# Two chunks of 96 tokens, casts of weights on GpSimd, packs formed turned, and new urgencies in a fused attention and MLP kernel

## The chip, the cores and the metric

The kernel runs on one core of a Trainium2 chip. The metric is the time of one launch on the device, in microseconds; the figure before is the median of three runs.

## The reference

Eight batches, eight heads, 576 tokens, head size 64, and 32 learned packs p per head. Attention runs twice: the packs attend to the tokens, which gives 32 packed vectors per head, and the tokens attend to those. Then comes an MLP over the 4608 tokens with the heads side by side (512 wide, 2048 inside):

```python
p_packed = sm_attn(p, k, v)               # softmax(p k^T / 8) v
out = sm_attn(q, p_packed, p_packed)      # softmax(q packed^T / 8) packed
x = out.transpose(0, 2, 1, 3).reshape(B * S, H * D)
h = x @ w_in
g = h * erf(softplus(h))
return g @ w_out
```

q, k, v and p are float32, the two weights float64 in memory.

## The kernel before

The kernel never forms x. With packs P and the token weights A of the second softmax, x @ w_in is A @ (P @ w_in): it makes "wp" = P @ w_in once for each batch and quarter of the 2048 columns (`w_prime`, `w_prime_first`), and then h = A @ wp, unit by unit; a unit is one batch and 128 of the 2048 columns (`h_unit`). To keep float32 precision at the fast rate, an operand is split into a high part (rounded to the fast float type) and a low part (the rest), and each product is three products: high x high, high x low, low x high. The tiles are named hi/lo, gh/gl, woh/wol, wph/wpl, a2h/a2l.

The first two batches run g @ w_out plainly, as units of "o". From the third batch on the same is done with fewer products by a scheme of sums and differences of blocks (`block`, products "c"), from parts of w_out that were formed before and kept in memory (`parts`).

The float64 weights are loaded as 16-bit words and turned into float32 in three steps (`convert`): GpSimd clears the target (L424), an engine casts the upper halves into it (L425 on ScalarE or L426 on VectorE, whichever comes first), and VectorE shifts the rest into place (L427). The staging tiles are wos (for w_out), wi and w_in. The first quarter of w_in comes in four pieces (`load_w_in_pair`): x says which half of the columns, and 2 * i which rows.

The first batch (`attention(0, ...)`, then `direct`) is the head of the kernel. Its order is: load p and k, queries, values; scores s of the packs (L421 called from `landed`); maximum and exponential; turn the weights (transposes, L699, L704) into tiles a1t and a1r; multiply them with the values (`gather`, tile p, 80 instructions); scale by the sums, transpose, copy: the packs pt (L738 to L743). The second scores (q against pt) follow, and `direct` handles their softmax in three parts of 256, 256 and 64 tokens.

What stands in which order is set by a planner in the kernel's own Python (`Program.order`). Every operation has a key, its urgency: where several are ready on an engine, the one with the lowest key goes first. The planner plays the whole program through with assumed durations, and the order that comes out is fixed for each engine's queue. Loads go to SyncE's queue, and they too are taken by lowest key, as far as there is room in their tiles. For the first batch the keys are -40 + i + PLAN["first"][i]: i = 0 for p and k, 1 for the values, 2 for the queries, 7 for the turns, 8 for the packs, 9 for the second scores, 10 to 13 for the parts of its softmax. A piece of w_in has the key of the values plus PLAN["first w"][2 * x + i].

At the end of `tile_pack_attention_moe` a loop fills TensorE's planned idle time before its operations with products of an identity matrix that nobody reads ("fill"), which are then part of TensorE's order. A wide one is two instructions of 512 columns.

The last block ends with two halves d = 0, 1: each is 12 products, one sum on VectorE (L1136) and two transfers, one on SyncE's queue and one on ScalarE's (L1141).

Of the kernel before, what the change touches and what calls it, by code (L numbers as in the profile page):

```python
# [14 lines left out]
F16 = mybir.dt.float16  # L15
BF16 = mybir.dt.bfloat16
# [5 lines left out]
PLAN = {  # L22
    "first": (-1655.04, -1082.68, -1274.99, 79.58, 0.0, 35.36, 16.66, 31.53, 72.43, 139.69, 67.61, -31.88, 85.8, 31.26),
    "wi by piece": (-162.72, 49.43, 320.21),
    "conv by piece": (89.72, -291.66, -190.3),
    "wo by group": (-551.62, -435.73, -397.6, -90.41, 49.67),
    "wo conv by group": (198.37, 226.24, -12.57, 1007.38, -374.69),
    "soon": (40.49, 61.86, -122.56, -117.47, -4.12, 109.39, 55.24, -94.6, 129.63, 109.4),
    "lag": 19.03,
    "act": -1381.6,  # L30
    "dve": -5.97,
    "copy": -21.32,
    "steady": (-77.6, 18.81, -15.19, -109.95, -11.8, 63.04, 10.58, -48.44, -142.04, 70.31, -139.34, -47.51, -66.75, 134.23),
    "second": (-53.98, -74.8, -47.15, -104.65, 87.68, -26.81, 73.19, -53.86, 5.68, -257.33, -25.4, 72.87, 198.79, -223.82),
    "third": (-46.13, 18.51, 43.92, 63.5, -111.16, 133.27, 18.45, 122.84, -270.72, 41.02, 42.6, -48.71, -122.17, -142.57),
    "wp": -78.11,
    "wi": 524.6,
    "wo": 108.98,
    "conv": -22.0,
    "rest": 27.37,  # L40
# [3 lines left out]
    "second half": 41.53,  # L44
    "wp first": (46.87, 23.46),
    "late": 1.436,
    "first w": (-34.02, 599.89, 20.85, -124.83),
    "also": {'top': -158.75, 'gate': 68.38, 'h': -0.92, 'cast': 81.65, 'taken': 21.33, 'h fast': -1157.74},
    "fill": (1.4, 60.0, 0.3, 0.4),
    "pad": (1.0, 0.0, 0.155, 0.079),  # L50
    "behind": 0.0,
    "first conv": (-145.98, -39.44, -15.82, -187.66),
# [3 lines left out]
    "split": 109.59,  # L56
# [12 lines left out]
    "gate": (-154.21, 1428.56, 1589.98),  # L69
    "copy fast": 34.59,  # L70
    "wp fast": -1007.0,
    "steady fast": (69.72, 75.09, 83.13, 101.05, 35.66, -202.52, -143.36, 7.84, -47.88, -22.2, -195.85, 216.61, -167.61, 61.46),
    "ml": (39.51, 1.95, 453.11),
    "sums ahead": (-103.94, 96.56, 110.02, -86.04, -59.16, -18.04, 88.79, 18.91, 4.56),
    "last ahead": (-78.59, -143.94, 85.03),
    "take": (14.93, -1376.66, -22.16),
    "fetch": -11.79,
    "st lead": (123.79, -10.21, 27.06, 147.95),
# [1282 lines left out]
```

## Time and profile before

| | us |
|---|---|
| median of 3 runs | 688.31 (687.78 to 689.96) |
| profiled execution | 687.53 |
| its span | 685.8 |
| TensorE busy | 674.9 (98%) |
| VectorE busy | 586.6 (86%) |
| ScalarE busy | 534.5 (78%) |
| GpSimd busy | 48.8 (7%) |

The span goes from the first to the last instruction of the profiled execution; its own time is that of the launch. Busy time counts an engine as soon as one of its instructions runs. For TensorE it holds the fillers too, and overlapping instructions count once. Idle time of an engine on which nobody waits costs nothing.

### The profile page before, as it was taken

To read this page: it belongs to the slowest core of one execution; us is meant where nothing else is said; L and a number is where in the kernel's file an instruction comes from. 1 tells how busy PE (TensorE), PEld (TensorE's weight loads), DVE (VectorE), ACT (ScalarE), POOL (GpSimd) and SP (SyncE) were. 2 spreads that over 40 slices of the span, in tenths; PEclk is the share of its full clock that TensorE was granted. 3 is DMA by queue.
4 is the path that set the end of the run, shared out by engine and by line. 5 is a ranking of instruction groups with operands and counts; after the bars stand their busy time and mean duration, and the time that the engine had idled before them with its cause. 6 is when DMAs were issued, how large, how long until landed. Compare 5 with 4: busy or idle time off the path is not lost.

```text
span 685.8 us, 15245 instructions
## 1 busy us (share of the span) xinstructions
PE 674.9 (98%) x5942; PEld 601.0 (88%) x5942; DVE 586.6 (86%) x990; ACT 534.5 (78%) x854; POOL 48.8 (7%) x67
## 2 busy tenths in 40 slices
PE   8999999999999999999999999999999999999997
PEld 4676778898769899898999989899998989999997
DVE  2899888978676899969999798969989699968995
ACT  2699699999369788877888787976889778868851
POOL 7200000001020000010001100011000100002000
PEclk9999999999999999999999999999999999999999
DMA  9999877997993796879769897779858787978973
GB/s 318 383 359 330 257 244 244 308 304 237 303 259 109 280 350 204 268 220 349 235 205 307 239 312 244 235 227 315 296 195 285 201 248 225 336 199 241 367 259 85
DMA packets 91288, 181.45 MB, mean 265 GB/s; under 512 B 16976, under 2 KB 46416, under 8 KB 91216
## 3 DMA queue, kind: packets, MB, share of 16 engines
q1 hardware_dynamic: 83904, 171.45, 73.1%
q0 software_dynamic: 6864, 8.29, 8.5%
q8 instruction: 47, 0.77, 0.5%
q10 hardware_dynamic: 448, 0.74, 0.3%
q14 instruction: 25, 0.20, 0.1%
HBM read 140.86 MB, written 39.58 MB: 263 GB/s over the span
## 4 chain that ended last, share of the span: by engine, by line
PE 86%; DVE 5%; ACT 3%; DMA 3%; issue 1%; POOL 0%; DVEq 0%; ACTq 0%; POOLq 0%
PE c L421 38%; PE h L421 26%; PE o L421 10%; PE wp L421 4%; PE s L421 3%; DMA wos<-w_out 2%; PE fill_ps_h L421 1%; PE p L421 1%; DMA wi<-w_in 1%; PE or L421 1%; PE t L699 1%; DVE gl L1030 1%; DVE hs L947 1%; DVE x L947 0%; ACT L942 0%
## 5 line engine op out<-in xcount | busy, mean ns | idle before, releaser
L421 PE MATMUL c<-gh,st 128*128 128x288 f32 x1344 | 286.1, 297 | 1.0 <-ACT obr L1165 0.7
L421 PEld LDWEIGHTS c<-gh,st 128*128 128x128 f32 x1344 | 220.7, 188 | 12.4 <-DVE cb L1088 3.9
L421 PE MATMUL c<-gl,st 128*128 128x288 f32 x672 | 198.2, 295 | 0.0
L421 PE MATMUL h<-a2h,wph 128*128 128x288 f32 (+2 forms) x512 | 154.7, 303 | 1.9 <-ACT hs L993 0.9
L421 PE MATMUL h<-a2l,wph 128*128 128x288 f32 (+2 forms) x512 | 150.6, 295 | 0.0
L421 PE MATMUL h<-a2h,wpl 128*128 128x288 f32 (+2 forms) x512 | 150.4, 294 | 0.0
L421 PEld LDWEIGHTS c<-gl,st 128*128 128x128 f32 x672 | 126.2, 188 | 0.0
L1030 DVE TENSOR_TENSOR gl<-x,gh 128x576 fp32r<-128x576 f32 x144 | 105.5, 749 | 3.4 <-ACT gh L1028 3.4
L421 PEld LDWEIGHTS h<-a2h,wph 128*128 128x128 f32 x512 | 95.9, 188 | 11.5 <-ACT hs L993 3.3
L421 PEld LDWEIGHTS h<-a2l,wph 128*128 128x128 f32 x512 | 96.1, 188 | 1.4 <-issue 0.5
L421 PEld LDWEIGHTS h<-a2h,wpl 128*128 128x128 f32 x512 | 96.2, 188 | 0.0
L1028 ACT CAST gh<-x 128x576 fp32r<-128x576 f32 x103 | 67.6, 672 | 35.6 <-PE c L421 30.5
L993 ACT COPY x<-h 128x288 f32<-128x288 f32 x117 | 46.6, 399 | 45.0 <-PE h L421 42.4
L995 DVE COPY x<-h 128x288 f32<-128x288 f32 x75 | 34.1, 454 | 29.4 <-PE h L421 29.0
L1097 POOL DMA_DIRECT2D out_t<-cb x21 | 25.4, 1208 | 444.9 <-DVE cb L1083 190.6
L1088 DVE TENSOR_TENSOR cb<-cb,c 128x576 f32<-128x576 f32 x59 | 44.2, 749 | 12.6 <-PE c L421 12.6
L421 PE MATMUL o<-woh,gh 128*128 128x512 f32 x120 | 48.0, 400 | 0.0
L421 PE MATMUL o<-woh,gl 128*128 128x512 f32 x120 | 46.9, 391 | 0.0
L421 PE MATMUL o<-wol,gh 128*128 128x512 f32 x120 | 46.8, 390 | 0.0
L942 ACT ACT_TABLE_LOAD x36 | 46.2, 1283 | 0.6
L937 ACT ACT_TABLE_LOAD x36 | 46.2, 1283 | 0.6
L1022 DVE TENSOR_TENSOR x<-x,x 128x576 f32<-128x576 f32 x48 | 35.8, 747 | 0.0
(430 smaller groups left out, 1078.7 us busy)
## 6 DMA issues: line engine op xcount, KB each, us to landing
st<-parts SPq DMA_DIRECT2D x167, 512.0 KB, 5.2
q<-qT SPq DMA_DIRECT2D x32, 288.0 KB, 5.8
k<-kT SPq DMA_DIRECT2D x30, 288.0 KB, 5.7
v<-v SPq DMA_DIRECT2D x32, 256.0 KB, 5.5
wos<-w_out SPq DMA_DIRECT2D x16, 511.8 KB, 5.0
out_t<-cb SPq DMA_DIRECT2D x26, 288.0 KB, 4.0
wi<-w_in SPq DMA_DIRECT2D x12, 511.8 KB, 6.1
out_t<-cb POOLq DMA_DIRECT2D x21, 288.0 KB, 6.4
```

The lines of the kernel that those rows point to most:

```text
L421: return nc.tensor.matmul(*args, **kw)
L699: return [nc.tensor.transpose(tbanks[x]()[:, (j % 2 * 2 + r) * P:(j % 2 * 2 + r + 1) * P], a[:, r, j * P:(j + 1) * P], ident[:]) for j in ...
L937: done.append(act(n + k0, S, lambda t=t, hs=hs: nc.scalar.activation(t[:], hs[:], AF.Softplus), (t,), (hs,), run="softplus", sb=True, kind ...
L942: erfs.append(act(e + k1 + i, S, lambda t=t: nc.scalar.activation(t[:], t[:], AF.Erf), (t,), (), run="erf", sb=True, kind=int(i < len(grou ...
L947: dve(key, S, lambda t=t, hs=hs: nc.vector.tensor_tensor(hs[:], t[:], hs[:], op=ALU.mult), (hs,), (t,))
L993: op = act(n + c / 2 - PLAN["copy" if b < NS else "copy fast"] + (PLAN["soon"][8 + (n > 7)] if n < 16 else 0), n1, lambda to=to, ps=ps, t0 ...
L995: also("h" if b < NS else "h fast", op, "DVE", dve_us(n1), lambda to=to, ps=ps, t0=t0, t1=t1, n1=n1: nc.vector.tensor_copy(to[:, t0:t1], p ...
L1022: dve(key, S, lambda: nc.vector.tensor_tensor(out[:], x[:], y[:], op=op), (out,), [t for t in (x, y) if t is not out])
L1028: op = act(key, S, lambda: nc.scalar.copy(hi[:], x[:]), (hi,), (x,), sb=True)
L1030: dve(key, S, lambda: nc.vector.tensor_tensor(lo[:], x[:], hi[:], op=ALU.subtract), (lo,), (x, hi))
L1088: dve(mk(s, 1) - PLAN["take"][one], S, lambda: nc.vector.tensor_tensor(two(out), two(x), to[:, :, 0:HT], op=ALU.add), (out,), (to,) if out ...
L1097: dma(mk(s, 1), P * S * 4, lambda: nc.gpsimd.dma_start(dst, two(t), accum_op=ALU.add), (), (t,), "POOL", after=[written[b, half, c]])
```

## The change

- The 576 tokens were cut into four chunks of 128 and one of 64 for the product with the values; now they are three of 128 and two of 96.
- In `convert` the cast of the upper halves can go to GpSimd: for quarters 1 to 3 of w_in and rows 2 to 15 of w_out. ScalarE is the other engine that may take it.
- In the first batch the weights are turned in three pieces, each as soon as its exponential is there. The product with the values is also formed turned (`gather_turned`, tile pq), which gives the packs already in the layout that the second scores need, without scaling. The scale by the sums goes into the copies of the second scores. The old form (`gather`) is kept for wp, with its key raised by "packs late".
- The identity is made by two instructions, of which the second is now the first in GpSimd's fixed order.
- The planner's start of the loads, their lateness, and the pace of the fillers (two paces) are set anew.
- The first half of the last sum is put ahead of the second half's products in the order of emission (`ahead`).
- The numbers of PLAN are new.

```diff
-    "first": (-1655.04, -1082.68, -1274.99, 79.58, 0.0, 35.36, 16.66, 31.53, 72.43, 139.69, 67.61, -31.88, 85.8, 31.26),
+    "first": (-1908.15, -1140.06, -1169.28, -122.78, 0.0, -54.09, 45.51, 65.33, -30.15, 122.75, 116.35, 23.39, 192.53, 145.43),
...
+    "packs late": 71.0,
+    "turned early": -112.1,
+    "by pool": (1, 2),
+    "pool lead": -185.41,
+    "pool other": 73.85,
...
-    "first w": (-34.02, 599.89, 20.85, -124.83),
+    "first w": (-24.06, -9.19, 29.08, -85.21),
-    "fill": (1.4, 60.0, 0.3, 0.4),
+    "fill": (2.0, 5.2, 50.0, 0.3, 0.4),
...
-        state = {"table": None, "within": False, "kind": 0, "bus": 2.3, "sent": 0}
+        state = {"table": None, "within": False, "kind": 0, "bus": 1.8, "sent": 0}
...
+            if op.ahead:
+                op.start = min(op.start, op.ahead.start - 1e-6)
...
+    LEFT = (S - (NT - 1) * P) // 2
+    CHUNKS = [(j * P, P) for j in range(NT - 1)] + [(S - 2 * LEFT, LEFT), (S - LEFT, LEFT)]
...
-    make_identity(nc, ident.t)
+    nc.gpsimd.memset(ident[:], 0.0)
+    line("POOL", nc.gpsimd.affine_select(out=ident[:], in_=ident[:], compare_op=ALU.not_equal, fill=1.0, base=0,
+                                         pattern=[[-1, P]], channel_multiplier=1))
...
+        if pool:
+            op = prog.add("POOL", key - PLAN["pool lead"], 0.25 + 0.00105 * n, 0.2, lambda: line("POOL", nc.gpsimd.tensor_copy(
+                dst().bitcast(F16)[:, 1::2], words().bitcast(BF16)[:, 2::4])), w, r)
+            op.other = ("ACT", PLAN["pool other"], act_us(n * 1.37, True), lambda: line("ACT", nc.scalar.copy(
+                dst().bitcast(F16)[:, 1::2], words().bitcast(BF16)[:, 2::4])))
...
+        pieces_of = ((0, 0, NT, (0, 0)), (1, 0, 2, (1, 0)), (1, 2, NT, (1, 1)))
...
+        if first:
+            for i, (r, j0, j1, part) in enumerate(pieces_of):
+                pe(keys[7] + i / 8, 0.11 * (j1 - j0), lambda r=r, j0=j0, j1=j1: [
+                    nc.tensor.transpose(tbanks[r]()[:, j * P:(j + 1) * P], a[:, r, j * P:(j + 1) * P], ident[:]) for j in range(j0, j1)],
+                   ((tw[r], part),), ([(a, 0)], [(a, (1, 0))], [(a, (1, 0)), (a, (1, 1))])[i] + [ident])
...
+            def gather_turned(j):
+                n = CHUNKS[j][1]
+                return [mm(turned[64 * r:64 * r + 64, NK * c:NK * c + NK],
+                           values[j][0:n, 64 * (2 * c + r):64 * (2 * c + r) + 64],
+                           at[0:n, j, r, NK * c:NK * c + NK] if j < NT else ar[0:n, r * P + NK * c:r * P + NK * c + NK],
+                           start=(j == 0 and c == 0), stop=(j == NCH - 1), skip_group_check=True)
+                        for c in range(NC) for r in range(2)]
+            for j in range(NCH):
+                pe(keys[8] + j / 8, V_US / 5, lambda j=j: gather_turned(j), (turned,),
+                   [(at, (0, 0)), (at, (1, j // 2)), values[j]] if j < NT else [ar, values[j]])
+            op = dve(keys[8], P, lambda: nc.vector.tensor_copy(early[:], turned[:, 0:P]), (early,), (turned,))
+            also("packs", op, "ACT", act_us(P), lambda: nc.scalar.copy(early[:], turned[:, 0:P]))
+            pe(keys[8] + PLAN["packs late"], V_US, lambda: gather(range(NCH)), ((w[0], "o"),),
+               [(at, part) for _, _, _, part in pieces_of] + [ar] + values)
+            keys = list(keys)
+            keys[8] += PLAN["packs late"]
...
-                act(keys[9] + x / 16, t1 - t0, lambda banks=banks, t0=t0, t1=t1, r=r: nc.scalar.copy(
-                    flat(ta)[:, 2 * t0 + r * (t1 - t0):2 * t0 + (r + 1) * (t1 - t0)], banks[r]()[:, 0:t1 - t0]),
-                    ((ta, (x, r)),), (w[r],))
+                act(keys[9] + x / 16, t1 - t0, lambda banks=banks, t0=t0, t1=t1, r=r: nc.scalar.activation(
+                    flat(ta)[:, 2 * t0 + r * (t1 - t0):2 * t0 + (r + 1) * (t1 - t0)], banks[r]()[:, 0:t1 - t0],
+                    AF.Copy, scale=sums[:, r:r + 1]), ((ta, (x, r)),), (w[r], (sums, r)))
...
+            op.ahead = halves.get(d + 1)
...
         while t + 0.112 < op.start - margin:
-            n = next((n for n in (4, 2) if t + 0.224 * n < op.start - margin - 0.5), 1)
+            one = 0.22 if t < slow else 0.112
+            n = next((n for n in (4, 2) if t + 2 * n * one < op.start - margin - 0.5), 1)
```

## Rows read from the trace of the kernel before

**Rows 1.** Busy us (instructions) by stretch: length, TensorE, weight load, VectorE, ScalarE, GpSimd; clock, DMA.
```profile
30.00:50.00 20.00, 18.87 (x247) 15.27 (x251) 18.63 (x48) 16.78 (x33) 0.46 (x1) 1.00 1.01 358
50.00:76.00 26.00, 25.48 (x180) 17.37 (x164) 25.39 (x40) 21.08 (x30) 0.00 (x0) 1.00 0.96 310
76.00:100.00 24.00, 23.27 (x180) 19.04 (x181) 19.53 (x38) 22.74 (x39) 0.00 (x0) 1.00 0.77 235
...
300.00:660.00 360.00, 360.00 (x3349) 340.70 (x3347) 320.84 (x514) 291.85 (x464) 21.73 (x18) 1.00 0.81 260
```

**Rows 2.** TensorE's timeline of the head: start, us, operation, count.
```profile
2.71 7.17 PE L421 MATMUL fill_ps_h<-ident 128*128 128x512 f32 x12 [2.71 <-POOL ident masks.py:199]
...
10.57 1.24 PE L421 MATMUL s<-k,p 64*32 64x288 f32 x32
...
18.94 1.21 PE L421 MATMUL s<-q,pt 64*32 64x256 f32 x32 [0.17 <-DVE pt L743]
...
30.03 0.38 PE L421 MATMUL h<-a2h,wph 128*128 128x256 f32 x1
```

**Rows 3.** Timeline of the tail, all engines.
```profile
681.49 0.82 DVE L1136 TENSOR_TENSOR cb<-cb,c 128x288 f32<-128x288 f32 x2 [2.44 <-PE c L421]
...
681.97 1.40 ACTq L1141 DMA_DIRECT2D out_t<-cb  x2
```

**Rows 4.** SyncE's queue in the head: start, us, transfers issued.
```profile
1.20 0.90 SPq L592 DMA_DIRECT2D k<-kT  x2
...
4.64 1.49 SPq L456 DMA_DIRECT2D w_in<-w_in  x2
6.18 3.46 SPq L611 DMA_DIRECT2D v<-v  x5
...
16.41 0.38 SPq L456 DMA_DIRECT2D w_in<-w_in  x1
```

**Rows 5.** Transfers issued from 1.15 to 2.1: count, KB each, us to landing.
```profile
k<-kT SPq DMA_DIRECT2D x2, 288.0 KB, 4.7
```

**Rows 6.** Transfers from 6.1 to 9.7: rate of all, and the fifth block of values.
```profile
DMA packets 696, 1.41 MB, mean 392 GB/s; under 512 B 64, under 2 KB 239, under 8 KB 696
...
v<-v SPq DMA_DIRECT2D x1, 128.0 KB, 7.3
```

**Rows 7.** Chain that ended last, its pieces up to 45 us: start, us, what.
```profile
16.33 1.46 PE p L421 x80
...
22.51 8.98 DMA wos<-w_out
...
31.56 0.77 ACT wo L425
```

**Rows 8.** What TensorE waited for from 28 to 100: total us, times, longest.
```profile
PE h L421 <- ACT a L682: 0.7, 1, 0.7
PE s L421 <- DVE wpl L892: 0.5, 1, 0.5
```

**Rows 9.** VectorE's timeline ahead of the first product.
```profile
28.13 0.67 DVE L427 SCALAR_TENSOR_TENSOR w_in<-wi,w_in 128x512 int32<-128x512 int32 x1
...
29.33 1.27 DVE L853 TENSOR_TENSOR a2l<-t,a2h 128x512 fp32r<-128x512 f32 x2
```

**Rows 10.** VectorE's casts from 20 to 140: count, busy us, mean ns, idle before.
```profile
L426 DVE CAST wo<-wos 128x512 f16<-128x512 bf16 x10 | 4.6, 462 | 0.7 <-DMA wos<-w_out 0.7
L426 DVE CAST w_in<-wi 128x512 f16<-128x512 bf16 x7 | 3.3, 465 | 1.6 <-DMA wi<-w_in 1.6
```

**Rows 11.** ScalarE's casts of the same stretch.
```profile
L425 ACT CAST w_in<-wi 128x512 f16<-128x512 bf16 x5 | 4.0, 791 | 1.1 <-DMA wi<-w_in 1.1
L425 ACT CAST wo<-wos 128x512 f16<-128x512 bf16 x5 | 3.9, 783 | 0.7 <-DMA wos<-w_out 0.7
```

**Rows 12.** Instructions on w_in up to 40 us: ns shortest, median, longest; starts.
```profile
L424 POOL MEMSET w_in<- x16: 515/524/781, 0.9 to 29.9; 128x512 f32 x16
...
L427 DVE SCALAR_TENSOR_TENSOR w_in<-w_in,w_in x4: 673/680/693, 15.4 to 28.7; 128x512 int32<-128x512 int32 x4
```

More of the change, by code (lines that the diff above doesn't have):

```diff
@@ L7 @@
 from concourse import mybir
-from concourse.masks import make_identity
 from concourse._compat import with_exitstack
@@ L43 @@
     "turns": (0, 8, 16),
-    "second half": 41.53,
-    "wp first": (46.87, 23.46),
-    "late": 1.436,
-    "first w": (-34.02, 599.89, 20.85, -124.83),
-    "also": {'top': -158.75, 'gate': 68.38, 'h': -0.92, 'cast': 81.65, 'taken': 21.33, 'h fast': -1157.74},
-    "fill": (1.4, 60.0, 0.3, 0.4),
-    "pad": (1.0, 0.0, 0.155, 0.079),
-    "behind": 0.0,
-    "first conv": (-145.98, -39.44, -15.82, -187.66),
+    "second half": -75.64,
+    "wp first": (-10.55, 55.44),
+    "late": 1.6,
+    "first w": (-24.06, -9.19, 29.08, -85.21),
+    "also": {'top': 39.37, 'gate': 64.57, 'h': 193.46, 'cast': -94.93, 'taken': 9.57, 'h fast': 32.66},
+    "fill": (2.0, 5.2, 50.0, 0.3, 0.4),
+    "pad": (1.0, 0.002, 0.147, 0.091),
+    "behind": 0.529,
+    "first conv": (96.7, 74.87, 16.53, -112.45),
     "k second": 'kvq',
@@ L148, in order @@
     def order(self):
+        for op in self.ops:
+            op.key += NUDGE.get(op.seq, 0.0)
         waits = {op: len(op.deps) for op in self.ops}
@@ L286, in order @@
                     state["bus"] = max(state["bus"], now + lead) + size / self.RATE[0]
-                    end = max(state["bus"], now + lead + size / self.RATE[1]) + tail + PLAN["late"] * (1.0 if op.way == "load" else 0.5)
+                    end = max(state["bus"], now + lead + size / self.RATE[1]) + tail + PLAN["late"] * (1.0 if op.way == "load" else 0.5) * min(1.0, now / 20)
                     if engine != "POOL":
@@ L710, in attention @@
                 pe(keys[7], T_US / 2, lambda x=x: turn(x), ((tw[x % len(tw)], x),), (a, ident))
-        if twhole:
+        if first:
+            for i, (r, j0, j1, part) in enumerate(pieces_of):
+                n = (j1 - j0) * P
+                dst = lambda r=r, j0=j0, j1=j1: at[:, j0:j1, r, :]
+                src = lambda r=r, j0=j0, j1=j1: tbanks[r]()[:, j0 * P:j1 * P].rearrange("p (j k) -> p j k", k=P)
+                op = act(keys[7] + i / 8, n, lambda dst=dst, src=src: nc.scalar.copy(dst(), src()), ((at, part),), ((tw[r], part),))
+                op.other = ("DVE", PLAN["turned early"], dve_us(n), lambda dst=dst, src=src: line("DVE", nc.vector.tensor_copy(dst(), src())))
+        elif twhole:
             act(keys[7], 1024, lambda: nc.scalar.copy(at[:].rearrange("p (x j) r k -> p x (j r k)", x=2), twhole()), (at,), tw)
@@ L732, in attention @@
         if first:
-            for j in range(NT):
-                pe(keys[8], V_US / 5, lambda j=j: gather((j,)), ((w[0], "o"),), ((at, j // 2), values[j]))
-            pe(keys[8], V_US / 5, lambda: gather((NT,)), ((w[0], "o"),), (ar, values[NT]))
+            turned = buf("ps_h", [P, 512], f"pq_{b}")
+            early = buf("pt", [P, P], f"pq{b}")
+            def gather_turned(j):
[14 more added lines that the diff above has]
+            keys[8] += PLAN["packs late"]
         else:
```

114 lines of the change are left out of this document (59 added, 55 removed).

## The prediction

> **What bounds the kernel now.** I read the busy time by stretches first, then TensorE's timeline of the first 31 us, the tail, and the loads of the head. Between 300 and 660 us TensorE is busy for 360.00 of 360 us [rows 1]. There nothing can be won: the products of that stretch stay as they are, and new urgencies can only keep it full or tear holes. What can be won lies at the two ends. Ahead of 30.03, where the first product of the MLP starts [rows 2], TensorE runs mainly filler products, which the kernel issues to keep it running. From 30 to 100 us it lacks 1.13 + 0.52 + 0.73 = 2.4 us [rows 1] (20 - 18.87, 26 - 25.48, 24 - 23.27), while VectorE is busy for 25.39 of 26 us. At the end the last sum starts at 681.49 [rows 3], and the span is over at 685.8.
>
> **The head.** The last part of k goes out by 2.1 at the latest [rows 4] and lands 4.7 later, at 6.5 to 6.8 [rows 5]. The scores start at 10.57, since the fillers placed ahead of them in TensorE's order run until then [rows 2]. The old plan counted 0.45 us for each of their twelve halves, from 1.4 on; they took 7.17 us and began at 2.71, behind the identity. The new plan starts at 2.0 and counts double up to 5.2, and the identity's select no longer stands behind other memsets. So the scores should start at about 6.7: 3.9 us earlier.
>
> Does that reach the end? The packs need the values. The five blocks go out from 6.18 to 9.64 [rows 4], the fifth at about 9.3, and it lands 7.3 later, at 16.6 [rows 6]. The 80 products with them run from 16.33 to 17.79 [rows 7], the last fifth from 17.5. So the late scores cost 0.9 us at most: behind the wait for the fillers stands a load that comes nearly as late. And by the keys it comes later still. SyncE sends the lowest key first. Before: queries -1313, second halves of w_in -1246.5, first halves -1155.7, values -1121.7, then -1100.8, and far behind -521.8. The trace has that order: two w_in, five values, and the last w_in at 16.41 [rows 4]. After: -1264.3, queries -1207.3, then -1203.1 and -1188.3, values -1179.1, and -1150.0. Three pieces of w_in stand ahead of the values instead of two: 511.5 KB more, 0.524 MB at 392 GB/s [rows 6] = 1.34 us. The last values land at about 17.9 (the last two blocks together are as large as before). What follows, a w_in, two w_out and four w_in pieces, moves by the same 1.34; TensorE waits for none of them directly [rows 8].
>
> With the values at 17.9 the last fifth of the turned products takes 0.3: 80 as before, half the columns and twice the weights each, so 0.7 to 2.9 us for all; I keep 1.46 as the nearest row. That gives 18.2. The turned packs save a multiply, a transpose and a copy (17.79 to 18.94, 1.15 us) and cost a copy of about 0.3. But the 80 products of the normalised packs have the key -62.15 + 71 = 8.85 and the second scores 91.75. They are ready with the same values, so they go first, and the second scores start at 18.2 + 1.46 = 19.7 instead of 18.94: 0.75 later. (If they went behind: 18.5, 0.4 earlier.) The scale in the four copies of the second scores: a tenth of a us at most; nothing.
>
> From there to the first product VectorE decides. The last step ahead of 30.03 is a low part begun at 29.33, behind two shifts of weights from 28.13, 0.60 each [rows 9]. One is of the w_in piece that now comes early, the other's cast goes to GpSimd and so comes later. Without both: -1.2. The first product comes at 30.03 + 0.75 - 1.2 = 29.6. **Head: -0.4**, bounds +1.5 (the shifts stay in the way, wide turned products) and -3.2 (first rival).
>
> **Casts on GpSimd.** 12 pieces of w_in and 14 of w_out may leave. Between 20 and 140 us VectorE did 17 casts at 0.46 [rows 10] and ScalarE 10 at 0.79, one or two of them of pieces that stay [rows 11]: some 7.9 us less on each. No row shows such a cast on GpSimd; the nearest is its memset of the same width, 0.52, at most 0.78 [rows 12], which only writes. Bounds 0.52 and 1.56; I take 0.8. It fits: 21 us in 120, and GpSimd is nearly idle there [rows 1]. The shift that follows on VectorE now waits for GpSimd instead; behind it stand the steps of the second batch. What TensorE gets from it: the gap of 0.9 at 32.6 hangs on the load of a w_out piece (22.51 to 31.5), for whose cast ScalarE stood still before it could empty a bank [rows 7]. That piece's cast leaves ScalarE, so the gap goes. The gap of 0.7 waits for the copy of the third batch's scores and stays, that of 0.5 for VectorE [rows 8]. I take 0.9 and half of the other 1.5: **-1.7**, bounds -2.4 and +2.8 (third rival).
>
> A shift of weights took 673 to 693 ns, beside memsets and without, while the memset stretched from 515 to 781 [rows 12]: GpSimd gave way, and I leave VectorE's times as they are. The Trainium skill (GPSIMD Engine Reference, Specifications) says that GpSimd's way to SBUF is shared with VectorE, contended by VectorE instructions in a two-port mode or with two SBUF inputs; by that VectorE could stand still during casts, which is the third rival. The same page (Performance versus the Vector engine) gives 769 ns measured for 512 elements of a simple loop; by it the 26 casts would take 20 us, next to my 21.
>
> **The tail.** Both halves of the last sum start only once TensorE is done, and ScalarE's queue then issues two transfers in 1.40 us [rows 3]. Placed ahead of the second half's products, the first half's sum can run near 680, and the last transfer goes out at 681.97 instead of 0.70 later. **-0.6**, bounds 0 and -0.8; if the second half's products had to wait for that sum, +0.5.
>
> **New urgencies after 100 us:** 0, as TensorE is full there; +1 at worst.
>
> **Sum**: -0.4 - 1.7 - 0.6 = -2.7. The profiled execution took 687.53 (the span and 1.7 around it): 684.8. It lies 0.78 under the median of 688.31, so the median after is 685.6.
>
> **Rivals.**
> - *The values do come first*, as the change's name says: two pieces of w_in behind them, 16.6 - 2.7 = 13.9, turned packs 14.2, normalised 15.7, so 3.2 earlier than 18.94. With middle and tail -5.5: 682.8. For it: then the scores' 3.9 us count. Against it: the keys, which give the order before correctly. 0.12.
> - *Nothing in the middle.* From 30 to 76 us the DMA engines and VectorE are full [rows 1]; what starts earlier waits later for weights, and the gaps come back elsewhere, the head's 0.4 too. Only the tail remains: 687.7. For it: the gaps are small and each waits for something else. Against it: one of them goes by name. 0.28.
> - *Slower: GpSimd stops VectorE.* If half of the 26 casts' 21 us stops VectorE, 10.5 come on against 7.9 saved: +2.6 on the chain that feeds TensorE up to 100 us; with the second scores 0.75 late and the tail's 0.6 it is +2.75: 691.1. It decides as soon as a shift beside a cast stretches beyond 1 us. Against it: the shifts beside memsets. The Trainium skill's rule on the shared way, named above, speaks for it. 0.15.
>
> **Chances.** The forecast has 0.45, its own range 683.5 to 687.2. A change under 0.3% (2.06 us) cannot be told from none. Under 686.25 lie seven tenths of the forecast, the first rival and a little of the second: 0.48; over 690.4 most of the third: 0.13; the rest is 0.39. The range cuts off the early half of the first rival and the late half of the third: 682.6 to 689.4.
>
> **What would show it.** Scores near 6.7; three w_in issues ahead of five values, the last of which lands near 17.9; 80 products twice in a row and second scores near 19.7; the first product near 29.6; casts of 0.8 on GpSimd beside shifts of 0.68; TensorE short by 1 us or less from 30 to 100; one half of the last sum near 680. Values landing before 15, shifts over 0.85, or a first product after 30.5 would make the forecast wrong.

## The result: 4.5 us slower, lost ahead of the second batch's scores

The changed kernel takes 692.91 us (median of 4 runs, 692.13 to 693.95), the kernel before beside it 688.45 (4 runs): ratio 1.0062, 95% interval 1.0049 to 1.0076. The forecast was 685.6 with a range up to 689.4: wrong, and on the other side. The profiled execution after took 693.95 with a span of 692.2, against 687.53 and 685.8 before. It is the slowest of its four, so the two profiles lie 6.4 us apart where the medians lie 4.5.

TensorE's timeline of the head after (start, us, operation, count, idle before); it answers to [rows 2]:

```profile
5.50 2.87 PE L436 MATMUL s<-k,p 64*32 64x288 f32 x32
...
17.97 0.66 PE L436 MATMUL pq<-a1r,v 96*64 96x32 f32 x16
18.56 1.10 PE L436 MATMUL p<-v,a1t 128*32 128x64 f32 x64
19.48 0.28 PE L436 MATMUL p<-v,a1r 96*32 96x64 f32 x2
21.81 0.65 PE L436 MATMUL p<-v,a1r 96*32 96x64 f32 x14 [2.05 <-issue]
22.39 1.11 PE L436 MATMUL s<-q,pq 64*32 64x256 f32 x16
...
37.38 0.72 PE L436 MATMUL s<-k,p 64*32 64x288 f32 x16
38.03 0.56 PE L436 MATMUL h<-a2h,wph 128*128 128x320 f32 x2
```

Up to 19.76 the order is as forecast: the scores start 5.1 us earlier (forecast 3.9), the last fifth of the turned products (pq) at 17.97, the normalised ones (p) behind it. Then, with 66 of their 80 instructions done, TensorE stands for 2.05 us "on issue": the profile shows no semaphore that holds it. The second scores (s<-q,pq) start at 22.39 instead of 18.94. The clock falls as well; columns as in [rows 1]:

```profile
20.00:21.00 1.00, 0.00 (x0) 0.00 (x0) 0.00 (x0) 0.00 (x0) 0.00 (x0) 1.00 1.00 393
21.00:22.00 1.00, 0.19 (x8) 0.19 (x11) 0.00 (x0) 0.00 (x0) 0.00 (x0) 0.55 1.02 409
22.00:23.00 1.00, 1.00 (x30) 0.44 (x24) 0.49 (x2) 0.00 (x0) 0.00 (x0) 0.50 1.05 418
...
28.00:29.00 1.00, 1.00 (x10) 0.90 (x9) 1.00 (x4) 0.56 (x2) 0.00 (x0) 1.00 0.50 142
```

During the idle time from 19.76 to 21.81, at 21.1, the granted clock falls to 0.50, the lower of the two levels (1.2 GHz), and it stays there until 27.9. So the second scores and the turns behind them run at half speed, and VectorE's first maximum starts at 26.23, 3.84 us after the second scores; before it was 21.20, 2.26 after 18.94.

From there VectorE works almost without a pause to 38.5 (its timeline, start and us first):

```profile
26.23 0.69 DVE L874 TENSOR_REDUCE mx<-s 128x16 f32<-128x512 f32 x1 [2.00 <-PE s L867]
26.84 0.97 DVE L448 SCALAR_TENSOR_TENSOR wo<-wos,wo 128x512 int32<-128x512 int32 x1
27.83 0.42 DVE L874 TENSOR_REDUCE mx<-s 64x8 f32<-64x256 f32 x1
...
29.16 0.67 DVE L874 TENSOR_REDUCE mx<-s 128x16 f32<-128x512 f32 x1
...
34.04 1.29 DVE L891 TENSOR_TENSOR tb<-tb,mx 128x512 f32<-128x512 f32 x2
...
36.65 0.68 DVE L904 TENSOR_TENSOR a2l<-t,a2h 128x512 fp32r<-128x512 f32 x1
...
37.85 0.68 DVE L904 TENSOR_TENSOR a2l<-t,a2h 128x512 fp32r<-128x512 f32 x1
```

The remainder of the tokens (64x256) and a shift stand between the two whole parts (128x512), and all three are divided one behind the other, from 33.4 on. The first product follows 11.8 us after the first maximum, not 8.8. But it isn't the first product that the end hangs on. Before, TensorE had done this much between its first product and the scores of the second batch:

```profile
30.03:35.34 5.31, 4.41 (x46) 1.00 1.05 346
```

That is 4.41 us of work, none of it filler: 24 products of h, 16 of wp and two turns. In the changed kernel the second batch's scores start at 37.38, 2.04 later, and of that work only the two turns are done. From the start of these scores to the end of the span TensorE does this (the first line is the kernel before, the second the changed one; length, busy, clock, DMA):

```profile
35.34:685.76 650.42, 643.65 (x5643) 1.00 0.82 260
37.38:692.17 654.79, 647.65 (x5675) 1.00 0.82 259
```

By the tiles that they write, the instructions that start in this stretch are the same in both kernels, but for 24 of h and 16 of wp more in the changed one. TensorE is busy for 4.00 us more and idle for 0.37 more. 2.04 + 4.00 + 0.37 = 6.41, the distance of the two spans. So nearly all of the loss is made by the start of these scores; later the two kernels differ by 0.4 us. In the stretches of [rows 1] the busy time alone hides it:

```profile
30.00:50.00 20.00, 19.13 (x158) 13.76 (x152) 19.65 (x47) 14.26 (x31) 3.60 (x4) 1.00 0.95 322
50.00:76.00 26.00, 26.00 (x258) 17.54 (x257) 23.67 (x38) 24.49 (x36) 4.74 (x6) 1.00 0.95 310
76.00:100.00 24.00, 23.35 (x180) 17.85 (x179) 21.92 (x36) 17.97 (x28) 3.90 (x5) 1.00 0.68 203
```

TensorE lacks 1.5 us from 30 to 100 instead of 2.4, but 6.1 us of its busy time from 30 to 50 are nothing but fillers, where before it was 0.6. From 100 to 300 it lacks another 1.59 (198.41 busy of 200) where before it was 0.68. At the end, against [rows 3]:

```profile
686.10 0.46 DVE L1188 TENSOR_TENSOR cb<-cb,c 128x288 f32<-128x288 f32 x1 [0.84 <-PE c L436]
...
686.61 0.54 PE L436 MATMUL c<-gh,st 128*128 128x288 f32 x2 [0.55 <-DVE cb L1188]
...
688.50 0.45 DVE L1188 TENSOR_TENSOR cb<-cb,c 128x288 f32<-128x288 f32 x1 [1.95 <-PE c L436]
```

The last sum stands 3.7 us ahead of the end instead of 4.3, but TensorE's second half waits 0.55 for the first half's sum.

### The profile page after: what moved, and what is told of

Same layout as the page of the kernel before. It is cut to its first block, busy times and chain, and to the rows that moved or that the text cites. A ratio compares the mean times of both kernels' runs of the same rounds, so it can differ in the third digit from the quotient of the medians.

```text
span 692.2 us, 15425 instructions
## 1 busy us (share of the span) xinstructions
PE 681.1 (98%) x6032; PEld 605.1 (87%) x6032; DVE 585.2 (85%) x972; ACT 531.0 (77%) x850; POOL 70.1 (10%) x90
## 4 chain that ended last, share of the span: by engine, by line
PE 78%; DVE 13%; DMA 3%; ACT 3%; issue 2%; SPq 0%; DVEq 0%; ACTq 0%
PE c L436 35%; PE h L436 24%; PE o L436 10%; PE wp L436 3%; DVE gl L1081 2%; PE s L436 2%; PE or L436 2%; PE p L436 1%; DVE x L1073 1%; DVE x L998 1%; DMA v<-v 1%; DMA q<-qT 1%; DVE hs L998 1%; PE t L722 1%; DVE cb L1140 1%
## 5 line engine op out<-in xcount | busy, mean ns | idle before, releaser
L1044 ACT COPY x<-h 128x288 f32<-128x288 f32 x137 | 54.7, 399 | 48.3 <-PE h L436 45.0
L1079 ACT CAST gh<-x 128x576 fp32r<-128x576 f32 x91 | 61.0, 671 | 29.0 <-PE c L436 27.4
L1046 DVE COPY x<-h 128x288 f32<-128x288 f32 x55 | 24.6, 449 | 34.7 <-PE h L436 34.5
```

The source lines that it names most:

```text
L1044: op = act(n + c / 2 - PLAN["copy" if b < NS else "copy fast"] + (PLAN["soon"][8 + (n > 7)] if n < 16 else 0), n1, lambda to=to, ps=ps, t0 ...
L1046: also("h" if b < NS else "h fast", op, "DVE", dve_us(n1), lambda to=to, ps=ps, t0=t0, t1=t1, n1=n1: nc.vector.tensor_copy(to[:, t0:t1], p ...
L1079: op = act(key, S, lambda: nc.scalar.copy(hi[:], x[:]), (hi,), (x,), sb=True)
```

## Experiments

They stand in five groups. In the first, three of the four edits go through the planner, which then orders the whole kernel anew. In the others ("order kept") the plan of the changed kernel, or of the one before, is made as it was, and only then are single operations given another place or another engine, or fillers left out:

```
+            op.start = MOVE.get(op.seq, op.start)
```

These landmarks are the base of the verdicts (us; from the traces, the last column the median of the runs; kernels before beside them 688.4 to 688.6):

| kernel | second scores | scores of batch 2 | span | span less these | median |
|---|---|---|---|---|---|
| before | 18.94 | 35.34 | 685.8 | 650.5 | 688.45 |
| before_early | 17.84 | 34.97 | 686.4 | 651.4 | 688.51 |
| before_pool | 19.31 | 34.99 | 687.1 | 652.1 | 688.86 |
| before_pool_act | 19.19 | 35.13 | 687.2 | 652.0 | 688.47 |
| after | 22.39 | 37.38 | 692.2 | 654.8 | 692.91 |
| narrow_fill | 21.46 | 35.91 | 691.0 | 655.1 | 692.30 |
| few_fill | 21.48 | 35.97 | 689.7 | 653.7 | 691.94 |
| values_frozen | 20.24 | 35.69 | 690.5 | 654.8 | 691.54 |
| scores_frozen | 19.41 | 35.27 | 688.0 | 652.7 | 691.51 |
| both_frozen | 18.93 | 35.37 | 690.5 | 655.1 | 692.25 |
| no_ahead | 21.98 | 36.20 | 689.5 | 653.3 | 692.36 |
| parts2_only | 22.78 | 37.71 | 693.4 | 655.7 | 693.86 |
| parts2_scores | 21.05 | 35.42 | 691.6 | 656.2 | 693.08 |
| parts_scores | 19.64 | 43.99 | 697.4 | 653.4 | 699.70 |
| parts_all | 18.19 | 45.01 | 698.2 | 653.2 | 700.58 |
| parts_frozen | 23.16 | 47.06 | 700.0 | 652.9 | 702.81 |
| casts_act | 22.63 | 37.15 | 699.2 | 662.0 | 700.54 |

Over a spread of 12 us the end follows the second batch's scores at 653 to 656; casts_act alone leaves that line. One trace is worth about 1 us: with the same order of sends the last values' product starts between 17.7 and 19.9, and no_ahead, whose head is that of the changed kernel, has the second batch's scores at 36.20 instead of 37.38.

### First group: one part undone, the rest planned anew

narrow_fill makes every filler 128 columns wide and changes no plan; values_first sends the values ahead, scores_first puts the normalised products behind the second scores, turned_undone takes the turned packs back to the old way.

```
-            n = next((n for n in (4, 2) if t + 2 * n * one < op.start - margin - 0.5), 1)
+            n = 1
```

> The kernel after with every filler narrow: the same filled time, but about 30 more products (60 more instructions with their weight loads) ahead of the turned packs. Theory of instructions: TensorE's 2.05 us without a wait, after the 66th of the 80 products of the normalised packs, is a wait for its next block of instructions, which crosses the full DMA engines. Then the hole keeps its place in the count of instructions: it comes 30 products earlier, after about the 36th, and ends 0.5 to 1.5 us earlier than 21.8 since the block is asked for earlier. Rival: the hole belongs to the operation (a tile, a bank, the values): it stays after the 66th. Time 691 to 693 by either.

Measured: 692.30, ratio 1.0049 (1.0034 to 1.0064). No hole, where the expectation had it 30 products earlier; instead the normalised products run at a granted clock of 0.50 from 19.2 on, and the second scores start 0.9 earlier. Within 0.6 us of the change.

```
-    "packs late": 71.0,
+    "packs late": 154.5,
-    ... + [ar] + values)
+    ... + [ar, early] + values)
```

> The kernel after with the normalised packs behind the second scores on TensorE (they wait for the copy of the turned packs; key raised). Theory of the head (values 1.3 late, normalised packs in front 0.9, hole 2.05, half clock after it 1.4, order of the softmax parts 2.3): second scores start near 19.0 instead of 22.4 and run at full clock; the hole falls into the normalised packs behind them; first product near 35 instead of 38.0; time 689.5 to 691. Rival (GpSimd's casts stop VectorE, the order on TensorE is hidden): first product and time as in the kernel after, 692 to 693.

Measured: 742.79, ratio 1.078 (1.0761 to 1.0800). TensorE in the head:

```profile
18.88 1.21 PE L436 MATMUL s<-q,pq 64*32 64x256 f32 x32
20.01 0.65 PE L436 MATMUL p<-v,a1t 128*32 128x64 f32 x32
21.51 0.66 PE L436 MATMUL p<-v,a1t 128*32 128x64 f32 x32 [0.85 <-issue]
```

The head did what the theory said: second scores 3.5 earlier at the full clock, first product at 31.27. And the hole has moved with the count: 80 turned instructions, 2 fillers, 32 of the second scores and 32 of the normalised ones are 146; in the changed kernel 80 + 66 are 146 (three fillers between the fifths are left out both times). So it's no wait of one product for its data; what it waits for stands in the last section. The rest was planned anew, and that costs 50 us: TensorE is busy for 16.25 of 20 us from 60, 40.79 of 50 from 250, 283.91 of 300 from 300.

```
-    "first w": (-24.06, -9.19, 29.08, -85.21),
+    "first w": (24.06, 9.19, 29.08, 85.21),
```

> The kernel after with all four pieces of w_in sent behind the first values. Theory of the head: the last values land near 13.9 instead of 17.9 and the turned packs are done near 14.6. If only the values count, second scores near 16 and the first product near 32: time 687 to 688.5. If the block of instructions is the next limit, TensorE stands still until 18 to 19 and the first product comes near 34: 689 to 690. Rival (middle or urgencies lose the time): the head shifts by 4 us and the time stays over 692.

Measured: 713.72, ratio 1.035 (1.0319 to 1.0381). Turned products from 11.89 to 15.8, first product at 33.2, and then 20 us lost later.

```
-            for j in range(NCH):
-                pe(keys[8] + j / 8, V_US / 5, lambda j=j: gather_turned(j), ...
+            for j in range(NCH):
+                pe(keys[8] + j / 8, V_US / 5, lambda j=j: gather((j,)), ((w[0], "o"),), ...
```

> The kernel after with the packs of the first batch formed as in the kernel before (80 products once, scaled, transposed, copied; no scale in the copies of the second scores). 160 instructions fewer ahead of the second scores. Theory of the head: no hole at 19.6, second scores at 17.9 + 0.3 + 1.15 = 19.4 or, behind the first wp, 20, at full clock; first product near 34.5: time 689 to 690.5. Rival (casts on GpSimd or the new urgencies lose the time): over 692.

Measured: 707.84, ratio 1.0277 (1.0247 to 1.0308). No hole with the 80 turned records gone, second scores at 19.78, first product at 31.8, and 15 us lost later. What follows for all three: planned anew, the kernel loses 15 to 50 us behind a head that is earlier, so their total times say nothing of the head. The next groups keep the order.

### Second group: the head moved, order kept

values_frozen sends the five value loads ahead of the four w_in pieces; scores_frozen puts the normalised products behind both halves of the second scores; both_frozen does both; few_fill leaves out the 21 narrow fillers ahead of 17 us.

```
+MOVE = {5: 3.96, ..., 9: 4.0, 22: 4.2, 10: 4.5, ...}   # v0 to v4, then w_in (values_frozen)
+MOVE = {58: 19.215, 59: 19.74, 60: 20.0, 61: 20.77, 101: 21.64}   # normalised products and what follows (scores_frozen)
```

> The changed kernel with its order kept to the letter after the head; only the head's sends are put otherwise: the five value loads go out ahead of all four w_in pieces (behind p, k and q), and the casts and shifts of those pieces stand behind what the values feed. Head theory: the last values land three pieces of about 1.3 us earlier, their product is at about 14 instead of 17.97, a hole of about 2 us stays at the same count of instructions (in the normalised packs), the second scores start near 18.5 instead of 22.4, the first product of the experts near 34 instead of 38.0, and the time falls by about 4 us to 688 to 690. Rivals: if the urgencies of the rest (or GpSimd beside VectorE) made the change slower, the first product comes earlier but the time stays at 691.5 to 693.5; if the pieces arrive late, wp00 waits for them and the first product stays above 37.

> The changed kernel with its order kept, except that the products of the normalised packs (and what follows from them: the division, the turn, the first wp product) stand behind both halves of the second scores. Head theory: the second scores start at 18.5 to 19.0, at the full clock, instead of 22.4, since the hole of about 2 us belongs to the count of TensorE instructions and now falls in the normalised packs, beside ScalarE's copies; the first product comes near 34.5 and the time is 688 to 690. If the hole were instead a wait of the normalised packs themselves (their data), the same would be seen, but the hole would stand at the 66th of their products again, not near the 30th. If urgencies or GpSimd are the cause: 691.5 to 693.5.

> Both of these: values sent ahead of the w_in pieces and the second scores ahead of the normalised packs, the rest of the order kept. Head theory: second scores at about 14.5 to 15.5, the first product near 30 to 31 (a little later than 8 us before 38.0, since wp and the keys of the second batch may now be the late ones), and 685 to 688, at or below the kernel before. If the head is not what the end hangs on (rivals: urgencies of the rest, GpSimd beside VectorE), 691 to 693.

> The changed kernel without its 21 narrow fillers (one product of 128 columns each) ahead of 17 us; the wide ones and everything else stay. Theory of the hole: it stands at a fixed number of TensorE instructions from the start (a block of code arriving late), so with some 80 instructions fewer ahead of it it leaves the normalised packs: they run through in about 1.8 us, the second scores start at about 20.0 and at the full clock, the hole falls into the second scores or the turns behind them, the first product comes 1 to 2 us earlier than 38.0 and the time is 690 to 692. Rival: the hole is a wait at a fixed place of the work (a landing, a bank): it stays at the 66th product of the normalised packs at 19.7 to 21.8 and nothing changes.

Measured: ratios 1.0044 (1.0027 to 1.0062), 1.0041 (1.0028 to 1.0054), 1.0048 (1.0029 to 1.0067), 1.0051 (1.0032 to 1.0070). They moved the second scores forward by 0.9 to 3.5 us and gave back 0.7 to 1.4 us, at the edge of what can be told from the change. few_fill came in as expected (690 to 692). The other three miss what the theory of the head promised, 688 to 690 for the first two and 685 to 688 for both_frozen. scores_frozen and both_frozen say most: the second batch's scores start at 35.27 and 35.37, as before the change (35.34), and yet the spans of these traces are 2.2 and 4.7 us longer than before, the medians 3.1 and 3.9 over the kernel before beside them. In both the 24 products of h and 16 of wp stand behind these scores. values_frozen shows in TensorE's timeline and in its loads why the values helped so little:

```profile
v<-v SPq DMA_DIRECT2D x2, 192.0 KB, 6.5
```

```profile
12.33 1.46 PE L438 MATMUL fill_ps_o<-ident 128*128 128x512 f32 x4
13.62 0.82 PE L1352 MATMUL fill_ps_h<-ident 128*128 128x128 f32 x6
14.37 0.66 PE L438 MATMUL pq<-a1t,v 128*64 128x32 f32 x16
...
17.13 0.64 PE L438 MATMUL pq<-a1r,v 96*64 96x32 f32 x16
```

The last values went out by 8.16 and took 6.5, so by this median they had landed by 14.7. But the fillers, placed by the plan's times for late values, run until 14.4 and between the fifths, and each fifth takes about 0.6 itself. (The expectation of parts_all below puts this down to shared bandwidth; that was wrong.) In scores_frozen the hole shrinks to 0.17, after 28 normalised records: 80 + 6 fillers + 32 + 28, again 146. In both_frozen there's none. With few_fill it leaves the normalised products, but TensorE, idle for 0.94 of 3 us from 16 to 19, is granted 0.50 from 17.9 to 21.4, and these products take nearly twice as long:

```profile
19.25 1.94 PE L436 MATMUL p<-v,a1t 128*32 128x64 f32 x64
```

### Third group: order of the softmax parts, order kept otherwise

The two whole parts go first, the remainder behind, and the first product is that of the first half. parts_scores adds scores_frozen to it, parts_all also the values right behind p and k.

```
+MOVE = {..., 80: 20.80, 70: 20.82, 81: 20.84, ..., 78: 24.2, 89: 24.25, ..., 470: 31.70, ...}
```

> The changed kernel, its order kept except in the first softmax: the two whole parts (128 token rows each half) go first on VectorE, ScalarE and TensorE, the rest of the tokens behind them, the shifts of weights after them, and the first product of the experts is the one of the first half (256 columns). Nothing ahead of the first maximum is touched. Theory: VectorE works without a pause from the first maximum (26.2) to the last low part (38.5) in the changed kernel, 12.3 us, where the kernel before had its first half done after 8.8; so with the old order of parts the first product comes at 35 to 36 instead of 38.0, and about half of that is kept at the end, as the four runs before showed (2 us at the first product gave 1.0 to 1.4): 690 to 691.5. Rival (only the hole and the late values count): the first product of the first half comes earlier, but the second half's products wait and the time stays at 692 to 693.

> The same order of parts, and the second scores ahead of the normalised packs too. Theory: first maximum near 22.2, first product 8.8 us later at about 31, as in the kernel before (30.0), and the time 688 to 690, within 0.3% of before. Rival (a loss in the middle of the plan of its own): first product at 31, yet 691 or more.

> The same two, and the five value loads sent right behind p and k, ahead of q and of all four w_in pieces. The run with values ahead of the pieces only showed that the transfers share the bandwidth: the last value landed 0.8 us earlier and not 4. With q behind as well, the last values land near 16 instead of 17.9, the second scores start near 17.5 if q has landed by then, the first maximum is near 20.5 and the first product near 29.5; time 686.5 to 689. If the shared bandwidth takes it back (q lands last), nothing is gained on the run before: 688 to 690.

Measured: 702.81, 699.70, 700.58 (ratios 1.0209, 1.0164, 1.0175, each within 0.0027). In parts_scores the first half's low part ends at 33.1, yet its product starts at 43.11:

```profile
35.27 2.07 PE L438 MATMUL fill_ps_h<-ident 128*128 128x512 f32 x2
37.14 1.49 PE L438 MATMUL fill_ps_o<-ident 128*128 128x512 f32 x2
38.46 4.46 PE L438 MATMUL fill_ps_m<-ident 128*128 128x512 f32 x10
42.76 0.60 PE L1352 MATMUL fill_ps_m<-ident 128*128 128x128 f32 x4
43.11 0.48 PE L438 MATMUL h<-a2h,wph 128*128 128x256 f32 x2
```

My own edit put eight microseconds of fillers there: in the plan the turns came at 24 and the product at 31.7, and fillers fill planned gaps whether or not the chip has them. They tell nothing on the parts, but they bear out the table's rule most clearly: the second batch's scores 6.6 to 9.7 later, the end 5.2 to 7.8 later. parts2 mends it: the product is planned right behind the turns, and fillers go only ahead of what is planned to start before 31 us (some stay: 1 us of them stands between the turns and the product in the trace of parts2_scores).

```
-    "fill": (2.0, 5.2, 50.0, 0.3, 0.4),
+    "fill": (2.0, 5.2, 31.0, 0.3, 0.4),
+MOVE = {..., 76: 25.9, 87: 25.91, ..., 470: 27.75, ...}
```

> The changed kernel, its order kept, except: second scores ahead of the normalised packs, whole parts first in the first softmax, ScalarE's weight casts of wp ahead of its exponentials, the first half's product right behind the turns, and no fillers after 25 us of the plan, so that none stand between the turns and that product (in the earlier run with the parts first, 8 us of fillers planned for a late product stood there). Theory (the head alone: 5 us up to the first maximum, 3 us from there to the first product): first maximum near 23, first product near 32 instead of 38.0, second half's product near 35, time 688 to 690, on the kernel before or up to 0.3% over it. Rival (the later order loses time of its own): first product near 32 and 691 or more.

> The same without moving the second scores: the hole and the half clock stay ahead of them. Theory: first maximum near 26.2 as in the changed kernel, first product 8.8 to 9.2 us later at about 35.2 instead of 38.0, time 690 to 692. Rival (order of the parts is worth nothing): 692 to 694.

Measured: 693.08, ratio 1.0071 (1.0054 to 1.0088), and 693.86, 1.0084 (1.0069 to 1.0099). The first product did come about 9 us after the first maximum (33.79 after 24.68, 36.07 after 26.62), as the theory had it, and it's worth nothing:

```profile
33.79 0.48 PE L438 MATMUL h<-a2h,wph 128*128 128x256 f32 x2
...
35.42 0.72 PE L438 MATMUL s<-k,p 64*32 64x288 f32 x16
...
38.95 0.39 PE L438 MATMUL h<-a2h,wph 128*128 128x256 f32 x1 [1.10 <-ACT hs L1046]
...
40.72 2.97 PE L438 MATMUL wp<-w_in,pt 64*32 64x512 f32 x16
```

One group of products (1 us) is done before the second batch's scores instead of the old four; then, in parts2_scores, TensorE waits 1.10 for ScalarE's copies, and the next wp takes 2.97 where it took 1.47 in the changed kernel. So in this order of the rest the order of the parts is worth nothing by itself.

### Fourth group: casts on GpSimd

casts_act emits every GpSimd cast of the changed kernel on ScalarE at the same place; before_pool gives all 26 late casts of the kernel before to GpSimd, before_pool_act the 9 that ScalarE had; orders kept.

```
+            if op.engine == "POOL" and op.other:
+                op.emit = op.other[3]
...
+            if getattr(op, "pool", None):
+                op.emit = op.pool
```

> The changed kernel with every cast that it gives to GpSimd put back on ScalarE at the same place of the order; nothing else differs. Theory (the head alone): the casts on GpSimd cost VectorE a few tenths each (a shift 0.97 and 1.13 us beside a cast instead of 0.68) and save ScalarE 0.7 us each, off the path: 691 to 693.5, as the changed kernel. Rival (GpSimd stops VectorE): the time falls to 688.5 to 690. Third: if ScalarE's time was on the path, it rises above 694.

> The kernel before, its order kept, with the upper casts of all 26 late weights (w_in from the second block, w_out from the third) on GpSimd, at the places of the order where ScalarE or VectorE had them. It tells whether this part of the change gains or loses without the change's head and urgencies. In the changed kernel putting the casts back on ScalarE cost 7.6 us; there the order was made for casts on GpSimd. Theory: VectorE is 95% busy from 20 to 80 us in the kernel before and loses 17 casts of 0.46 (7.9 us over the run), ScalarE 9 of 0.79; beside a cast of 0.77 a two-input operation of VectorE is stretched by up to 0.3 to 0.45, so about half is kept in the early stretch: 685.5 to 688.5. Rival (GpSimd stops VectorE, and its casts wait for landings in turn and hold the memsets behind them): 689 to 693. Third: no difference within 0.3%, since TensorE is idle for only 3.1 us in all from 20 to 300 us.

> The same for the 9 casts alone that the kernel before gives to ScalarE; VectorE keeps its 17. Theory: ScalarE is off the path except around 31.5, where a cast that waits for its landing holds the copy that TensorE waits for (0.90 us at 32.6); that wait goes: 687 to 688.5. Rival: the stretch of VectorE's two-input operations beside the casts takes it back: 688.5 to 690.

Measured: 700.54, ratio 1.0171 (1.0149 to 1.0193); 688.86, 1.0004 (0.9995 to 1.0013); 688.47, 1.0004 (0.9995 to 1.0013). So casts_act can't tell what GpSimd's casts cost: in this order ScalarE, which now makes them, is late itself. TensorE's waits from 38 to 200 us are on ScalarE and on VectorE (total, times, longest), and VectorE in turn waits for ScalarE's casts:

```profile
PE h L438 <- ACT hs L1046: 1.7, 4, 0.7
PE h L438 <- DVE hs L1048: 1.6, 3, 0.7
PE o L438 <- DVE gl L1010: 1.1, 2, 0.6
...
DVE w_in L450 <- ACT w_in L445: 4.8, 3, 1.9
```

In the order of the kernel before GpSimd's casts change nothing. The wait that the prediction named (0.9 for hs at 32.6, [rows 7]) does go in before_pool, and others come; its waits from 30 to 100:

```profile
PE h L423 <- ACT a L686: 0.7, 1, 0.7
PE o L423 <- DVE gh L958: 0.7, 1, 0.7
PE o L423 <- DVE gl L961: 0.5, 2, 0.3
PE h L423 <- ACT a1r L725: 0.3, 1, 0.3
```

2.2 us in place of 0.9 + 0.7 + 0.5 + 0.2 = 2.3.

### Fifth group: the scores alone, the tail alone

before_early is the kernel before with the identity made by itself and the early fillers paced anew; no_ahead is the changed kernel without `op.ahead`.

```
+            one = 0.22 if t < slow else 0.112
...
-            op.ahead = halves.get(d + 1)
```

> The kernel before, its order kept, with two parts of the change alone: the identity is made without the wait behind GpSimd's clearing, and the fillers ahead of the scores are paced at twice the planned time, so that the scores start as soon as the keys have landed (near 6 instead of 10.57). Theory: the packs wait for the last values (16.3 to 17.7) in any case, so the 4 us at the scores are hidden: second scores at 18.9 as before, and 688 to 689, no difference. Rival (earlier scores help by themselves): second scores earlier and 685 to 687.

> The changed kernel without the one part at its end: the last sum of the first half is emitted behind the second half's products again. Theory from the trace: with the part, the tail from the last sum to the end is 0.6 us shorter (3.7 for 4.3), but TensorE's second half waits 0.55 us for the bank that the sum reads; without it both go, and the time is the changed kernel's within 0.3 us: 692 to 693.5. Rival (the part helps by 0.6, as the prediction had it): 693.3 to 694.

Measured: 688.51, ratio 1.0001 (0.9989 to 1.0013), and 692.36, ratio 1.0068 (1.0051 to 1.0085); both times as expected. In before_early the scores start at 8.28, not at 6 as expected, and the second scores at 17.84 instead of 18.94, but at a granted clock of 0.50 (18 to 21 us); they take 2.17 us instead of 1.21, and the gain doesn't reach the end. The tail's part is worth nothing. In no_ahead the last sum starts 4.3 us ahead of the end (span 689.5), 0.6 us more than with the part, and TensorE doesn't wait:

```profile
685.25 0.82 DVE L1188 TENSOR_TENSOR cb<-cb,c 128x288 f32<-128x288 f32 x2 [2.44 <-PE c L436]
```

No version beats the kernel before; the nearest to it among the changed ones are scores_frozen and values_frozen (691.51 and 691.54).

## Why the prediction was wrong, step by step

- **Order on SyncE, last values, normalised packs in front** (17.9): right. The products stand in that order and the last fifth at 17.97; that it fits to 0.1 is luck, as it starts anywhere from 17.7 to 19.9 with these sends. The first rival was rightly small. The scores came at 5.50, not 6.7, which is worth nothing, as the prediction said and before_early bears out.
- **Second scores at 19.7:** failed, 22.39. Of the 2.7 us the hole is 2.05, which the sum had no term for; the rest is the half clock on the 14 products behind it, and the turned fifth at 0.59 where the sum had 0.3 (80 of them take 3.0 us, five times 0.6: twice the 1.46 taken, just over the upper bound of 2.9).
- **"From there to the first product VectorE decides: -1.2", 29.6:** this is the step that failed most. Measured 15.6 us from the second scores to the first product, 9.9 forecast, 11.1 before. 1.6 more than before lie ahead of the first maximum, where TensorE turns at half clock, and 3.0 behind it in VectorE's new order of parts. It looked only at which shifts leave, not at the changed urgency of the second half (41.53 to -75.64), which moved all parts in front of the first division (the code says so; no run took this number back). It also took the wrong mark: parts2_only and parts2_scores brought the first product 2 and 4.2 us forward for nothing. What counts is when the second batch's scores start and how much work is done by then: they start 2.04 late with 4.00 us of work undone. So the head, forecast at -0.4, costs about 6.0 in these two traces. In scores_frozen and both_frozen, where the second batch's scores are on time in the trace, 3.1 and 3.9 us of loss are left by the medians.
- **Middle -1.7:** failed. The named gap goes, as before_pool shows, and as much comes elsewhere. This is the second rival's mechanism. TensorE's 1.5 us short from 30 to 100 in the changed kernel (1 or less was forecast) can't be counted as a gain, as its busy time from 30 on is mostly fillers until 37.4.
- **GpSimd stops VectorE:** the rival whose time, 691.1, was nearest, for the wrong reason. There is some of it; the shift at 26.84 above took 0.97 instead of 0.68. Two casts of GpSimd's timeline of the changed kernel, and a second such shift of VectorE's:

```profile
26.55 0.77 POOL L441 CAST w_in<-wi 128x512 f16<-128x512 bf16 x1 [1.38 <-DMA wi<-w_in]
...
43.85 1.16 POOL L441 CAST wo<-wos 128x512 f16<-128x512 bf16 x1 [2.41 <-DMA wos<-w_out]
...
96.10 1.20 DVE L448 SCALAR_TENSOR_TENSOR w_in<-wi,w_in 128x512 int32<-128x512 int32 x1
```

  The shortest cast takes 0.77, as forecast; 23 went to GpSimd, and their mean is 868 ns (9 of w_in) and 989 ns (14 of w_out). The prediction's signs against itself, a shift over 0.85 and one beyond 1 us, both came: 0.97 at 26.84 and 1.20 at 96.10. But they are two of 28; the other 26 took 0.69 or less. The mean shift rose from 681 to 722 ns for w_in (12) and from 685 to 697 for w_out (16), 0.7 us in all, and before_pool, with all 26 casts on GpSimd, loses nothing. (The 1.13 in the expectation of casts_act isn't a shift but a low part of w_out, at 44.37.)
- **Tail -0.6:** failed at the point that its bound named (+0.5): 0.61 won, 0.55 lost by TensorE's wait for the first half's sum.
- **Urgencies 0 after 100 us, +1 at worst:** inside the bound. TensorE is idle for 1.59 us from 100 to 300 instead of 0.68, and over all that follows the start of the second batch's scores for 0.37 more.

Not settled: what makes the loads of the head scatter by 2 us, and why runs with the second batch's scores equally early end 1 to 4 us apart. Why the work left undone can't be had back is open too: parts2_scores put 6 of the 24 products of h in front of these scores and won nothing, and no run put all of them and the 16 of wp there, or left out the 5.6 us of fillers that stand from 30 to 37.4 instead. And the account holds for two single traces, 6.4 us apart; the medians are 4.5 apart.

## What to carry to other kernels

Ask of an early stage not when its first result comes but what the bound engine has done by the time the next stage starts: here seven edits with the order kept brought the first product 1.4 to 4.2 us forward, and the end moved between 1.4 earlier and 1.0 later. Fillers and orders that are written from planned times are part of the critical path as soon as the chip runs late or early; move the work and the fillers must move too. When an order comes from a planner, change the emission behind it first: three edits that helped the head by 5 to 7 us cost 15 to 50 us when the whole was planned anew.

## What the hardware showed that I had not expected

**A hole where the code comes late.** TensorE stops, and no semaphore holds it. In all eleven runs that have it, the hole stands after the same number of instructions from TensorE's first one on, fillers included: 223 products, each with its weight load (222 in values_first), whatever comes next. And its end keeps a fixed distance to a packet of code: in the changed kernel one packet of 0.02 MB moves on an instruction queue between 19.25 and 19.50 (columns: packets, MB, share of 16 engines),

```profile
q8 instruction: 1, 0.02, 27.1%
```

and the products go on at 21.81, 2.5 us after its start. In the ten other runs the same packet stands 2.3 to 2.5 us ahead of the restart: 17.5 and 19.88 in values_frozen, 19.0 and 21.40 in no_ahead, 18.9 and 21.35 in scores_frozen, 16.0 and 18.43 in values_first, 20.5 and 22.80 in parts_frozen. In both_frozen it comes at 17.6, TensorE reaches the place after 20.4, and there is no hole; so it is in narrow_fill (17.1 and 20.1). The loads moved some 400 GB/s all the while. What sets the time of the packet isn't shown. The Trainium skill (Runtime: NRT & Kernel Launch, Instruction fetch mechanics) says that an engine's instructions are fetched in blocks of 16 KiB while the block before runs, and that crossing a block costs little, "mostly hidden"; the runs agree with the blocks (the packet holds 16,384 bytes) and show a case where the cost is not hidden: up to 2.27 us, in a burst of tiny products under loads that fill the DMA engines.

**The idle time costs twice, but not always, and the clock falls without it too.** The granted clock was 0.50 from 21.1 to 27.9 in the changed kernel, from within the 2.05 us of idle time on; in values_frozen, after 0.99 us, it stayed at 1.00. In narrow_fill, which has no hole, it was 0.50 from 19.2 to 22.6 although TensorE, with the products of the packs, was busy for 0.97 of the us from 18 to 19. So the hole alone doesn't explain the lower clock.
